# Score products of 512 columns into two sums, with three shared PSUM banks instead of four

## The chip, the cores and the metric

The kernel runs on one core of a Trainium2 chip. The metric is the device time of one execution in microseconds (us), the median of several runs. A profiled execution beside them shows the work of each engine: PE (TensorE), whose weight loads are listed as PEld, DVE (VectorE), ACT (ScalarE), POOL (GpSimd), and SP, which only issues transfers here.

## The reference

For each of four batches, q, k and v are 6336 rows of 256 channels. The columns of q and k are normalised over the rows, a 256 by 256 score matrix is formed, its softmax is applied to v, and a gated convolution of five taps follows.

```python
qn = q / (np.linalg.norm(q, axis=1, keepdims=True) + 1e-06)
kn = k / (np.linalg.norm(k, axis=1, keepdims=True) + 1e-06)
s = kn.transpose(0, 2, 1) @ qn / tau          # 256 x 256 a batch
s = s - s.max(-1, keepdims=True)
a = np.exp(s)
a /= a.sum(-1, keepdims=True) + 1e-09
x = v @ a
# gate: a causal convolution of x over five rows, a weight for each tap and channel
gate = 1.0 / (1.0 + np.exp(-gate_pre))
val = x @ w_val
out = gate * val @ w_out
```

All of it is float32.

## The kernel before

There are two kinds of work, and they run interleaved. The **score side** of a batch reads q and k in groups of three row tiles (128 rows each). For most groups each number is split into a high part (`hi`, rounded to the fast float32r format of the PE, by ACT) and a low part (the rest, by POOL), and the score is summed on the PE from three products of 256 columns for each row tile and each half of the channels: high times high, high times low, low times high. A few early groups skip the split and use slower float32 products of the raw data. ACT squares the rows, and DVE and POOL add the squares up (`acc`, L214) for the norms. The sum of the scores is one PSUM tile, `s_ps`, opened by a product with zeros (`clear`, L231).

The **value side** works on chunks of 508 rows (the last one of a batch has 240), 52 steps in all. A step transposes a chunk of v on the PE (`t_ps`, two tiles), which ACT and DVE split into `v_hi` (L336) and `v_lo` (L337); multiplies it with the softmax weights (`x_ps`, two tiles), from which ACT and then DVE form the five taps of the gate (L359, L361); takes the sigmoid (L367); multiplies it with softmax times `w_val` (`val_ps`, two tiles), which DVE multiplies into the gate (L374); splits that again (L387, L388), multiplies it with `w_out` (`o_ps`, two tiles) and copies the result out (L414). Each step of the pipeline works for a different chunk: in one turn the PE computes `val_ps` of a chunk, `x_ps` of the next, `t_ps` of the one after, and `o_ps` of the one before.

When a batch's scores are complete, `softmax` (L236 on) runs as a chain of small instructions on PE, ACT and DVE between those of the value side. Its tile of norms, called `o_ps` as well (L245), stays in use until the reciprocal of the exponentials' sum (L272). For batch 2 its first product starts at 337.94 us and that reciprocal at 356.86 us.

**PSUM** has eight banks. Before the change `s_ps` holds one, the running sums `acc_ps` one, `x_ps` two, and the other four are shared in turn (tag "bank") by `t_ps`, `val_ps`, `o_ps` and the tiles of softmax. A tile takes a bank that is free again, so its first product waits until the last reader of the tile that had this bank is done.

The order of the work on each engine is set when the kernel is built, by a scheduler that weighs the instructions by a model of their times. Each engine then executes its own list strictly in that order. Any edit to pools or tiles makes new lists.

## Time and profile before

| | |
|---|---|
| median of 3 runs | 657.26 us (657.15 to 657.44) |
| the profiled execution's own time | 658.18 us |
| its span, first to last instruction | 656.3 us |
| PE busy | 637.8 us, 97% of the span |
| DVE, ACT, POOL busy | 80%, 71%, 55% |
| score products of split parts (L226) | 852 of 256 columns |

A line of the profile that groups instructions names the source line, engine, operation, the tiles as out<-in, the shape and the count; behind the first bar stand the busy time in us and the mean duration of one in ns, and behind the second the idle time of that engine just before them and what ended it. Products on the PE are pipelined: the duration of one is longer than the distance from its start to the next one's, and it is the distance that the PE pays.

### The profile page before, as it was taken

The page shows a single profiled execution, that of the slowest core. Times are in us where ns is not written, and L with a number is a line of the kernel's source. Part 1 is how long each engine was busy: PE and PEld are TensorE (multiplying, and loading weights), DVE is VectorE, ACT ScalarE, POOL GpSimd, SP SyncE. Part 2 cuts the span into 40 slices and gives each one's busy share as a digit, 9 for nine tenths or more (in the row PEclk, how much of TensorE's full clock was granted, in tenths as well). Part 3 has the DMA queues.
Part 4 walks back from the last instruction along what each step waited for, and adds up shares of the span by engine and source line. Part 5 has one row for each costly group of instructions (what it writes and reads, how often), then busy time and mean ns, then how long its engine had stood idle before and what let it go on. Part 6 is the DMA issues. An engine that isn't in the chain of part 4 may idle for free.

```text
span 656.3 us, 10656 instructions
## 1 busy us (share of the span) xinstructions
PE 637.8 (97%) x4008; PEld 571.1 (87%) x4008; DVE 523.0 (80%) x832; ACT 466.1 (71%) x607; POOL 360.8 (55%) x173
## 2 busy tenths in 40 slices
PE   7989999999999999999998999999999999999996
PEld 5868799989979999999997998998999798888886
DVE  3898689787878688778788688778778888888894
ACT  4565978867888768668698687767777756655564
POOL 2442796965837769659565497766763222312220
PEclk9999999999999999999999999999999999999999
DMA  8999874555635565545564365563222343443213
GB/s 268 322 328 337 267 225 152 161 166 165 179 103 176 188 195 176 173 132 170 175 184 121 109 217 158 189 185 104 65 78 71 118 126 95 121 129 104 65 50 100
DMA packets 107875, 105.75 MB, mean 161 GB/s; under 512 B 5744, under 2 KB 107312, under 8 KB 107824
## 3 DMA queue, kind: packets, MB, share of 16 engines
q1 hardware_dynamic: 81520, 79.24, 39.0%
q10 hardware_dynamic: 26304, 25.84, 13.9%
q8 instruction: 31, 0.51, 0.3%
q14 instruction: 20, 0.16, 0.1%
HBM read 79.11 MB, written 25.95 MB: 160 GB/s over the span
## 4 chain that ended last, share of the span: by engine, by line
PE 85%; ACT 5%; DVE 4%; POOL 2%; DMA 2%; issue 1%; SPq 1%; ACTq 0%; POOLq 0%
PE o_ps L404 20%; PE x_ps L345 20%; PE val_ps L345 19%; PE s_ps L226 18%; PE t_ps L335 6%; POOL hi L193 1%; ACT sq L209 1%; PE o_ps L294 1%; DMA raw<-in_k_dram 1%; DVE acc_ps L214 1%; ACT hi L192 1%; DVE gate L361 1%; DMA v_raw<-in_v_dram 1%; DVE gate L374 1%; ACT gate L367 0%
## 5 line engine op out<-in xcount | busy, mean ns | idle before, releaser
L361 DVE SCALAR_TENSOR_TENSOR gate<-x_ps,wa,gate 128x508 f32<-128x508 f32 (+1 forms) x416 | 275.4, 716 | 15.7 <-ACT gate L359 14.6
L193 POOL TENSOR_TENSOR hi<-raw,hi 128x1536 fp32r<-128x1536 f32 (+2 forms) x54 | 167.8, 3110 | 94.5 <-ACT hi L192 94.5
L388 POOL TENSOR_TENSOR g_lo<-gate,g_hi 128x1016 fp32r<-128x1016 f32 (+1 forms) x50 | 116.6, 2332 | 145.2 <-ACT g_hi L387 130.6
L214 DVE TENSOR_TENSOR acc_ps<-acc_ps,sq 128x512 f32<-128x512 f32 (+1 forms) x134 | 93.4, 697 | 74.8 <-ACT sq L209 71.6
L345 PE MATMUL x_ps<-v_hi,w 128*128 128x512 f32 (+1 forms) x416 | 139.1, 394 | 0.0
L345 PE MATMUL val_ps<-v_hi,w 128*128 128x508 f32 (+1 forms) x416 | 133.9, 383 | 0.8 <-ACT o_sb L414 0.7
L226 PE MATMUL s_ps<-hi 128*128 128x256 f32 (+1 forms) x852 | 121.1, 287 | 7.4 <-ACT hi L192 4.0
L226 PEld LDWEIGHTS s_ps<-hi 128*128 128x128 f32 (+1 forms) x852 | 110.7, 190 | 13.9 <-ACT hi L192 5.5
L404 PE MATMUL o_ps<-wo_hi,g_hi 128*128 128x256 f32 x400 | 113.2, 283 | 1.7 <-ACT g_hi L383 1.5
L414 ACT COPY o_sb<-o_ps 128x512 f32<-128x512 f32 x99 | 58.2, 589 | 79.1 <-PE o_ps L404 77.9
L404 PE MATMUL o_ps<-wo_lo,g_hi 128*128 128x256 f32 x400 | 112.1, 280 | 0.0
L404 PE MATMUL o_ps<-wo_hi,g_lo 128*128 128x256 f32 x400 | 111.7, 280 | 0.0
L209 ACT ACTIVATE sq<-raw 128x1536 f32<-128x1536 f32 (+3 forms) x69 | 96.0, 1393 | 16.5 <-DVE acc_ps L214 7.9
L214 POOL TENSOR_TENSOR acc<-acc,sq 128x512 f32<-128x512 f32 x58 | 76.4, 1318 | 39.7 <-ACT sq L209 39.3
L345 PEld LDWEIGHTS x_ps<-v_hi,w 128*128 128x128 f32 x416 | 78.2, 190 | 14.3 <-DVE gate L361 0.2
L345 PEld LDWEIGHTS val_ps<-v_hi,w 128*128 128x128 f32 x416 | 77.1, 188 | 14.5 <-ACT o_sb L414 0.9
L359 ACT ACTIVATE gate<-x_ps,wa 128x508 f32<-128x508 f32 (+1 forms) x104 | 68.2, 671 | 20.5 <-PE x_ps L345 20.2
L336 ACT CAST v_hi<-t_ps 128x512 fp32r<-128x512 f32 (+1 forms) x104 | 55.8, 569 | 36.2 <-PE t_ps L335 36.2
L345 PE MATMUL x_ps<-v_lo,w 128*128 128x512 f32 (+1 forms) x208 | 80.2, 386 | 0.0
L345 PE MATMUL val_ps<-v_lo,w 128*128 128x508 f32 (+1 forms) x208 | 79.2, 381 | 0.0
L374 DVE TENSOR_TENSOR gate<-val_ps,gate 128x508 f32<-128x508 f32 (+1 forms) x104 | 64.3, 657 | 18.3 <-ACT gate L367 14.0
L404 PEld LDWEIGHTS o_ps<-wo_hi,g_hi 128*128 128x128 f32 x400 | 75.2, 188 | 3.1 <-ACT g_hi L383 1.7
(84 smaller groups left out, 799.3 us busy)
## 6 DMA issues: line engine op xcount, KB each, us to landing
raw<-in_q_dram SPq DMA_DIRECT2D x64, 384.0 KB
raw<-in_k_dram SPq DMA_DIRECT2D x64, 384.0 KB
v_raw<-in_v_dram SPq DMA_DIRECT2D x44, 512.0 KB
out_dram<-o_sb ACTq DMA_DIRECT2D x48, 384.0 KB
out_dram<-o_sb ACTq DMA_DIRECT2D x48, 124.0 KB
v_raw<-in_v_dram SPq DMA_DIRECT2D x4, 384.0 KB
raw<-in_q_dram SPq DMA_DIRECT2D x4, 128.0 KB
raw<-in_k_dram SPq DMA_DIRECT2D x4, 128.0 KB
```

The source lines that it names most:

```text
L193: nc.gpsimd.tensor_tensor(hi[r, js, :, 1, :], raw[r, js, :, :], hi[r, js, :, 0, :].bitcast(F32), ALU.subtract)
L209: nc.scalar.activation(sq[0:np_, ja:jb], raw[0:np_, ja:jb], AF.Square)
L214: eng.tensor_tensor(st[key][0:np_], st[key][0:np_], sq[0:np_, j], ALU.add)
L226: nc.tensor.matmul(st["s"][:, h, :], lhs, rhs, start=False, stop=stop and h == NH - 1 and n_ == len(ops) - 1)
L336: nc.scalar.copy(th[:, h, 0:w], tp[:, 0:w])
L345: nc.tensor.matmul(ps, wt[:, which, ws, ch, hs], vs[:, ch, lo:hi_], start=n_ == 0, stop=n_ == 3 * NH - 1)
L359: nc.scalar.activation(gate[:, h, 0:w], x_ps[:, 0:w], AF.Copy, scale=cw[:, h, 0:1])
L361: nc.vector.scalar_tensor_tensor(gate[:, h, 0:w], x_ps[:, tap:tap + w], cw[:, h, tap:tap + 1], gate[:, h, 0:w], ALU.mult, ALU.add)
L374: nc.vector.tensor_tensor(gate[:, h, 0:w], val_ps[:, 0:w], gate[:, h, 0:w], ALU.mult)
L388: nc.gpsimd.tensor_tensor(gl[:, :, 0:w], gate[:, :, 0:w], gh[:, :, 0:w].bitcast(F32), ALU.subtract)
L404: nc.tensor.matmul(o_ps[:, u * C:(u + 1) * C], gs[:, h, off:off + P], ws[:, h, :], start=n_ == 0, stop=n_ == 3 * NH - 1)
L414: marks["ACT"] = nc.scalar.copy(o_sb[:, j:j + len(pair), :], o_ps[:, 0:len(pair) * C].rearrange("p (j c) -> p j c", c=C))
```

## The change

The two products that share the high half of k become one: `hi` of k is loaded once and multiplied with 512 columns, the high and the low part of q side by side. Its result goes to 512 columns of a sum, the first half holding high times high, the second high times low. The low part of k times the high part of q, 256 columns, is added to the first half. So each half of the channels now has a bank of its own, `s_ps` holds two banks instead of one, and the shared pool has three instead of four. `clear` becomes two products. At the end ACT copies the second half out, as it copied the whole before, and one new DVE instruction adds the first half to it. The handle that is kept in `marks["PE"]` is overwritten by softmax before it is read.

```diff
-    ps = ctx.enter_context(tc.tile_pool(name="ps", bufs=4, space=PSUM))
+    ps = ctx.enter_context(tc.tile_pool(name="ps", bufs=3, space=PSUM))
...
-                s=ps_s.tile([P, NH, C], F32, name="s_ps"),
+                s=ps_s.tile([P, NH, 2 * C], F32, name="s_ps"),
...
-                    ops = [(hi[r, j, 1, x, hs], hi[r, j, 0, y, :]) for x, y in ((0, 0), (0, 1), (1, 0))]
+                    ops = [(hi[r, j, 1, 0, hs], hi[r, j, 0, :, :].rearrange("p x c -> p (x c)")),
+                           (hi[r, j, 1, 1, hs], hi[r, j, 0, 0, :])]
                 for n_, (lhs, rhs) in enumerate(ops):
-                    nc.tensor.matmul(st["s"][:, h, :], lhs, rhs, start=False,
-                                     stop=stop and h == NH - 1 and n_ == len(ops) - 1)
+                    marks["PE"] = nc.tensor.matmul(st["s"][:, h, 0:rhs.shape[1]], lhs, rhs, start=False,
+                                                   stop=stop and n_ == len(ops) - 1)
...
-            nc.tensor.matmul(st["s"].rearrange("p h c -> p (h c)"), zeros[:, 0:P], zeros, start=True, stop=False)
+            for h in range(NH):
+                nc.tensor.matmul(st["s"][:, h, :], zeros[:, 0:P], zeros, start=True, stop=False)
...
-        nc.scalar.copy(s, st["s"])
+        nc.scalar.copy(s, st["s"][:, :, C:])
+        nc.vector.tensor_tensor(s, st["s"][:, :, 0:C], s, ALU.add)
```

The scheduler makes new lists from this. Three places of them follow; the numbers in the names tell the tiles apart, and "waits" names the engines whose signals an instruction waits for (DMAHW is a transfer). Line numbers of the changed kernel stand up to three higher behind the edits.

The first place is the PE in a step amid the scores of batch 2. Before the change, the two transposed tiles (2949 and 2956) of a step stand one behind the other, ahead of the step's `x_ps`:

```order
L345 MATMUL val_ps_2935<-v_hi_2699,w_1876 128x508
L335 MATMUL t_ps_2949<-ident_96,v_raw_2746 128x128 [waits DMAHW1_49,Activation_49]
L335 MATMUL t_ps_2949<-ident_96,v_raw_2746 128x128 x3
L335 MATMUL t_ps_2956<-ident_96,v_raw_2746 128x128 [waits Activation_49]
L335 MATMUL t_ps_2956<-ident_96,v_raw_2746 128x128 x3
L345 MATMUL x_ps_2903<-v_hi_2823,w_1876 128x512 [waits DVE_49]
```

In the changed kernel the second one (2813) comes after both `x_ps` and ten of the twelve score products of a group:

```order
L227 MATMUL s_ps_1616<-hi_2750 128x256
L227 MATMUL s_ps_1616<-hi_2750 128x512
L227 MATMUL s_ps_1616<-hi_2750 128x256
L338 MATMUL t_ps_2813<-ident_96,v_raw_2615 128x128 [waits DVE_49]
L338 MATMUL t_ps_2813<-ident_96,v_raw_2615 128x128 x3
L227 MATMUL s_ps_1616<-hi_2750 128x512
L227 MATMUL s_ps_1616<-hi_2750 128x256
L407 MATMUL o_ps_2821<-wo_hi_111,g_hi_2682 128x256 [waits DVE_49]
```

The score products now alternate between 512 and 256 columns, and some of them stand between the first transposed tile and the second.

The second place is the PE during the softmax of batch 1, where the tile of norms (o_ps_1628) holds one of the three banks. Here both transposed tiles and then `o_ps` follow one another directly:

```order
L227 MATMUL s_ps_1616<-hi_1619 128x512
L227 MATMUL s_ps_1616<-hi_1619 128x256
L338 MATMUL t_ps_1690<-ident_96,v_raw_1453 128x128 [waits DMAHW0_49,DVE_49]
L338 MATMUL t_ps_1690<-ident_96,v_raw_1453 128x128 x3
L338 MATMUL t_ps_1697<-ident_96,v_raw_1453 128x128 [waits DVE_49]
L338 MATMUL t_ps_1697<-ident_96,v_raw_1453 128x128 x3
L407 MATMUL o_ps_1707<-wo_hi_111,g_hi_1520 128x256 [waits DVE_49]
L407 MATMUL o_ps_1707<-wo_lo_112,g_hi_1520 128x256
```

Before, the first transposed tile stood some 25 products earlier at this place, and with four banks `o_ps` had another bank to take than those of the two. With the norms in one of three, the tiles 1690 and 1697 take the other two, and o_ps_1707 takes the bank of 1690.

The third place is DVE at the same time in the changed kernel, from the second multiplication of the gate (`val_ps`) to the two `v_lo` that read the transposed tiles:

```order
L377 TENSOR_TENSOR gate_1479<-val_ps_1667,gate_1479 128x508 [waits PE_49]
L261 RECIPROCAL o_ps_1628<-o_ps_1628 128x256 [waits DVE_49]
L364 SCALAR_TENSOR_TENSOR gate_1633<-x_ps_1634,wa_109,gate_1633 128x508 [waits Activation_49]
L263 TENSOR_SCALAR nk_1678<-o_ps_1628,rtau_107 128x2 [waits DVE_49]
L364 SCALAR_TENSOR_TENSOR gate_1633<-x_ps_1646,wa_109,gate_1633 128x508 [waits Activation_49]
L364 SCALAR_TENSOR_TENSOR gate_1633<-x_ps_1634,wa_109,gate_1633 128x508 [waits DVE_49]
L266 SCALAR_TENSOR_TENSOR s_1610<-s_1610,nk_1678,o_ps_1628 128x256 [waits DVE_49]
L266 SCALAR_TENSOR_TENSOR s_1610<-s_1610,nk_1678,o_ps_1628 128x256
L364 SCALAR_TENSOR_TENSOR gate_1633<-x_ps_1646,wa_109,gate_1633 128x508 [waits DVE_49]
L340 TENSOR_TENSOR v_lo_1689<-t_ps_1690,v_hi_1688 128x512 [waits Activation_49]
L364 SCALAR_TENSOR_TENSOR gate_1633<-x_ps_1634,wa_109,gate_1633 128x508 [waits DVE_49]
L340 TENSOR_TENSOR v_lo_1689<-t_ps_1697,v_hi_1688 128x512 [waits Activation_49]
```

Four taps, a reciprocal over 256 columns, two scalings of the scores and one small instruction stand between that multiplication and the first `v_lo`. In the softmax of batch 2 these are three taps and the row minimum (L268), in that of batch 3 one small instruction, three taps, two scalings and the row minimum; at both places the PE's list has the same order as above, two transposed tiles and then two `o_ps`.

## The prediction

> **What bounds the kernel now.** I read the page's engine totals and its chain first, then the stretches between and during the softmaxes, then the waits inside those.
>
> ```profile
> PE 637.8 (97%) x4008; PEld 571.1 (87%) x4008; DVE 523.0 (80%) x832; ACT 466.1 (71%) x607; POOL 360.8 (55%) x173
> PE 85%; ACT 5%; DVE 4%; POOL 2%; DMA 2%; issue 1%; SPq 1%; ACTq 0%; POOLq 0%
> ```
>
> The PE is busy nearly all the time, and 85% of the chain that ended last is its own work. So every us taken from its list counts, and so does every wait put into it. The table of stretches (start:end, length, then busy time of PE, PEld, DVE, ACT, POOL, granted clock, DMA) tells where it waits:
>
> ```profile
> 100.00:180.00 80.00, 80.00 (x532) 72.87 (x531) 66.05 (x102) 62.58 (x77) 57.36 (x25) 1.00 0.54 160
> 215.00:330.00 115.00, 115.00 (x778) 105.66 (x778) 92.00 (x146) 84.67 (x104) 80.02 (x35) 1.00 0.55 167
> 360.00:490.00 130.00, 130.00 (x868) 119.13 (x867) 101.18 (x161) 96.86 (x119) 90.05 (x40) 0.99 0.46 139
> 545.00:640.00 95.00, 95.00 (x580) 84.43 (x579) 83.18 (x128) 54.73 (x83) 26.41 (x11) 1.00 0.33 96
> 180.00:215.00 35.00, 34.21 (x214) 29.78 (x214) 28.93 (x50) 29.48 (x43) 20.59 (x9) 1.00 0.52 153
> 330.00:360.00 30.00, 27.31 (x172) 24.41 (x171) 24.10 (x42) 26.97 (x38) 17.82 (x9) 0.97 0.57 164
> 490.00:525.00 35.00, 33.75 (x204) 29.34 (x203) 29.63 (x50) 26.31 (x41) 11.75 (x6) 1.00 0.33 94
> ```
>
> The first four stretches lie between softmaxes and after the last: the PE never rests. The last three hold the softmaxes of batches 1, 2 and 3: 0.8, 2.7 and 1.25 us of rest. These are the sensitive places, since the norms occupy a shared bank there.
>
> **The products.** An instruction's price on the PE is the distance between starts:
>
> ```profile
> 299.62 2.43 PE L226 MATMUL s_ps<-hi 128*128 128x256 f32 x19
> 301.89 0.28 PE L404 MATMUL o_ps<-wo_hi,g_hi 128*128 128x256 f32 x1
> 302.01 0.28 PE L404 MATMUL o_ps<-wo_lo,g_hi 128*128 128x256 f32 x1
> ...
> 310.48 0.40 PE L345 MATMUL x_ps<-v_hi,w 128*128 128x512 f32 x1
> ...
> 313.01 0.40 PE L345 MATMUL x_ps<-v_hi,w 128*128 128x512 f32 x1
> ```
>
> Nineteen products of 256 columns take 301.89 - 299.62 = 2.27 us, 0.1195 each. Between the first and the last of the quoted run of twelve products of 512 columns lie eleven distances, 313.01 - 310.48 = 2.53 us, 0.230 each. Three of 256 cost 0.3585, one of 512 and one of 256 cost 0.3495: 0.009 us saved per triple. The number of columns stays the same; only a fixed part of one instruction goes. The 852 products are 284 triples: **-2.5 us** (0 if the 512 columns cost as two of 256). In the Trainium skill, the section "Wait — 56ns, not 53.3ns?" of "TensorE: Matmul & The Clock Gate" gives a fixed cost of about 2.5 ns per product, by which the saving would be 284 x 2.5 ns = 0.7 us, an estimate from that page. The rows here show a larger fixed part, and I keep theirs.
>
> `clear` gains one product of 512 columns in each batch: 4 x 0.230 = **+0.9 us**.
>
> **The new addition on DVE** reads PSUM and 512 elements per partition, as these do:
>
> ```profile
> L240 DVE TENSOR_TENSOR acc_all<-acc_ps,acc 128x512 f32<-128x512 f32 x4 | 2.7, 682 | 0.1
> PE s_ps L231 <- ACT s L242: 0.7, 1, 0.7
> PE val_ps L345 <- ACT o_sb L414: 0.7, 1, 0.7
> ```
>
> Four times 0.68 us. The next batch's `clear` must now wait for it instead of ACT's copy. Before, the PE waited for that copy once for 0.7 us (the second row), after batch 0, where little else is ready: there the addition is on the path, **+0.7 us**. In the other three softmaxes value-side products cover `clear`; without that cover each would cost up to 0.68 us more, 2 us in all.
>
> **The bank in the steady steps.** A step asks for six shared tiles, and before the change a fourth bank was in use when the second `t_ps` came. The new list puts both `x_ps` and ten score products (4.5 us) ahead of it, so `val_ps` has that long to be read. The step's DVE work is shorter than the step (92.00 us of 115.00 in the second stretch), so I take 0 for the steps with scores. After 545 us there are no score products to put between, and DVE is busy 83.18 of 95 us. There the second `o_ps` product group follows right when the second multiplication of the gate ends; I take 0.1 us for each of 12 steps, **+1 us**, between 0 and 6 (0.5 each, about one instruction of DVE).
>
> **The bank during softmax** is the main term. With the norms in one bank two are left. The PE's list has t, t, o, o, so the first `o_ps` waits for the first `v_lo`, on the bank of the first `t_ps`; and that `t_ps` waits for the multiplication that reads `val_ps`. Between that multiplication and `v_lo`, DVE works through the items in its list while the PE has only the rest of two transposes. Before, the DVE list of batch 2 has the same items here:
>
> ```profile
> 350.06 1.28 DVE L374 TENSOR_TENSOR gate<-val_ps,gate 128x508 f32<-128x508 f32 x2 [0.30 <-ACT gate L367]
> 351.26 0.74 DVE L361 SCALAR_TENSOR_TENSOR gate<-x_ps,wa,gate 128x508 f32<-128x508 f32 x1
> 351.91 0.68 DVE L265 TENSOR_REDUCE m<-s 128x2 f32<-128x512 f32 x1
> 352.51 1.39 DVE L361 SCALAR_TENSOR_TENSOR gate<-x_ps,wa,gate 128x508 f32<-128x508 f32 x2
> 353.82 0.68 DVE L337 TENSOR_TENSOR v_lo<-t_ps,v_hi 128x512 fp32r<-128x512 f32 x1
> L258 DVE RECIPROCAL o_ps<-o_ps 128x256 f32<-128x256 f32 x4 | 7.1, 1763 | 0.1
> L263 DVE SCALAR_TENSOR_TENSOR s<-s,nk,o_ps 128x256 f32<-128x256 f32 x8 | 3.5, 473 | 0.0
> L260 DVE TENSOR_SCALAR nk<-o_ps,rtau 128x2 f32<-128x2 f32 x4 | 0.8, 208 | 0.0
> 585.74 1.03 PE L335 MATMUL t_ps<-ident,v_raw 128*128 128x128 f32 x8
> 586.53 0.48 PE L345 MATMUL x_ps<-v_hi,w 128*128 128x512 f32 x1
> ```
>
> The columns of a timeline row are start and duration in us. From the end of the second multiplication (350.06 + 1.28 = 351.34) to the end of `v_lo` (353.82 + 0.68 = 354.50) pass 3.16 us: three taps, the row minimum, `v_lo`. Eight transposes take 586.53 - 585.74 = 0.8 us, 0.4 a tile.
>
> - Batch 2, the same items: 3.16 us, of which the PE fills 0.4 with the second `t_ps`: 2.7 us of waiting.
> - Batch 3 adds the small instruction and the two scalings: 3.16 + 0.21 + 0.95 = 4.3, less 0.4: 3.9 us.
> - Batch 1 has a fourth tap (about 0.7, half of the 1.39 us of two), the reciprocal, the small instruction and the scalings, and no row minimum: 3.16 + 0.7 + 1.76 + 0.21 + 0.95 - 0.68 = 6.1. Adding up the PE's list, the PE gets to its first `t_ps` when the second multiplication ends, so both transposes lie inside: 5.3 us.
>
> Together **+11.9 us**. Batch 0 has no `o_ps` group at its softmax, so 0 there. In the list of before nothing waits here: the first transposed tile is written earlier and a fourth bank is free for `o_ps`. From below this term is bounded by 0, if `v_lo` were ready when the PE comes; from above by the same waits without any transpose beside them, 13.6 us.
>
> **Further waits** follow in the same stretches, since the softmax tiles go on using banks. In batch 1 a transposed tile of the next step waits for a multiplication that stands behind an addition of squares, for which ACT must first cast a whole group:
>
> ```profile
> L192 ACT CAST hi<-raw 128x1536 fp32r<-128x1536 f32 x44 | 65.0, 1479 | 0.0
> ```
>
> One such wait in each of the three, a cast and a reader, is 1.48 + 0.68 = 2.2 us, 6.5 in all. The rest of 4.75 us that the PE had in these stretches will partly fall into them; I count half of it off: **+4 us**, between 0 and 9.
>
> **The clock.** Before, one long rest of the PE was followed by slow products:
>
> ```profile
> 354.89 0.28 PE L404 MATMUL o_ps<-wo_hi,g_lo 128*128 128x256 f32 x1
> 357.86 0.53 PE L226 MATMUL s_ps<-hi 128*128 128x256 f32 x1 [2.69 <-ACT hi L192]
> 358.19 0.63 PE L345 MATMUL x_ps<-v_hi,w 128*128 128x512 f32 x1
> 358.62 0.63 PE L345 MATMUL x_ps<-v_lo,w 128*128 128x512 f32 x1
> 358.00:361.50 3.50, 3.50 (x9) 2.78 (x10) 1.72 (x3) 3.47 (x5) 3.50 (x2) 0.52 0.36 90
> ```
>
> After 2.69 us of idleness the granted clock is 0.52 for about 3.5 us and a product of 512 columns takes 0.43 us instead of 0.23: 3.5 x 0.48 = 1.7 us lost. The new rests of batches 1 and 3 are longer than that one, so two more such spells are likely, 3.4 us, part of which falls before another wait: **+2 us**, between 0 and 3.4. The Trainium skill, in Part 1 of "TensorE: Matmul & The Clock Gate", puts the clock back to half after an idle window of about 3.4 us that runs freely; by that the rest of batch 2 need not slow anything and those of batches 1 and 3 may. The trace shows it after 2.69 us, and I go by the trace.
>
> **Sum**: -2.5 + 0.9 + 0.7 + 1 + 11.9 + 4 + 2 = +18 us. The profiled execution's own time is 658.18 us (its span of 656.3 and 1.9 around it), which gives 676.2. It lies 0.9 us above the median of the runs shown, so the forecast for the median is **675.3 us**, 2.7% slower.
>
> **Rivals.**
>
> *The lists cover the missing bank.* The scheduler placed `t_ps` elsewhere in the steady steps, and if the PE comes late to those `o_ps`, behind other waits, `v_lo` is done. Then only the products and `clear` count: 657.26 - 2.5 + 0.9 = 655.7 us, 0.2% faster. It decides if fewer than two instructions of DVE stand in front of `v_lo` when the PE arrives. For it: before, the PE never rests over 325 us between softmaxes in which banks are shared too, and its one listed wait for a shared bank is 0.7 us (the last row with the addition). Against it: the lists have four to eight instructions there, and the PE's list has nothing between. Chance 0.08. If the addition and the 512-column products are a little dearer than I think, the same case ends within 0.2% (about what a measurement of this kernel can tell from no change): 0.04.
>
> *The waits are there but half as long*, because the PE reaches the transposes later, behind waits for POOL's low parts, and the long rests then cause no slow clock: -2.5 + 0.9 + 0.7 + 6 + 1 = +6 us, 663.4 us. For it: two of the three stretches already have rests of their own. Against it: a later PE comes later to everything. Chance 0.13.
>
> *The bank is short in every step.* If a `val_ps` is read later than its next tile is due, each turn slips. For it: after 545 us DVE has only 12 of 95 us free, and a `t_ps` takes the bank of a `val_ps` there. Against it: the PE list gives 4.5 us of other products. At half a us in each of 46 steps it is 23 us on top of the sum: 698 us. Chance 0.06.
>
> *The change does not do what it says*: it does, as the rows of the lists show 512 and 256 columns in turn; a 512-column product that costs two of 256 would raise the sum by 2.5 us and nothing else.
>
> **How the numbers follow.** The sum has 0.69, its own range from the lower and upper ends of its terms is 664 to 686 us. With the milder case taken in from below and some of the steady one from above, 661 to 688 holds 8 in 10. Slower by over 0.2%: 0.69 + 0.13 + 0.06 = 0.88; the same: 0.04; faster: 0.08.
>
> **What would show it.** In the profile after, the group of L227 should hold 284 products of 512 columns and 284 of 256; the stretches between softmaxes should stay without rest of the PE. The waits should list `o_ps` L407 on the PE as ended by DVE `v_lo` L340, three times with 2.5 to 5.5 us, each in a softmax, and two more spells of half clock. The prediction is wrong if these waits are below 1 us, if the PE rests in the steady steps, or if the whole loss sits at the addition L245 and the `clear` behind it.

## The result and the profile after

The changed kernel takes **686.78 us** (median of 4 runs, 685.12 to 688.84), against 657.26 before: a ratio of 1.0459 as recorded, with a 95% interval of 1.0436 to 1.0482 (the two medians alone divide to 1.0449). The forecast was 675.3 us with a range of 661 to 688. So the direction was right and the time lies just inside the range, 11.5 us above the forecast. It lies above the 664 to 686 us that the prediction gave as the range of its sum alone. The profiled span grew from 656.3 to 684.2 us, by 27.9.

The totals of the engines and the chain that ended last, after:

```profile
PE 648.0 (95%) x3728; PEld 560.2 (82%) x3728; DVE 526.0 (77%) x836; ACT 470.9 (69%) x607; POOL 360.3 (53%) x173
PE 66%; DVE 11%; ACT 11%; issue 4%; SPq 3%; DMA 2%; POOL 2%; ACTq 1%; DVEq 0%
```

The PE's own share of the chain fell from 85% to 66%, and DVE's rose from 4% to 11%: the end is no longer set by the PE's work alone but by work that the PE waits for. The products themselves changed as described. The groups of L227, shapes kept apart:

```profile
L227 PE MATMUL s_ps<-hi 128*128 128x512 f32 x280 | 104.3, 406 | 6.0 <-POOL hi L193 6.0
L227 PE MATMUL s_ps<-hi 128*128 128x256 f32 x280 | 78.5, 280 | 0.0
```

(Four more of each cover 64 rows, so there are 284 of each, as forecast.) The stretches after, cut at the starts of the steps (columns as in the table of the prediction):

```profile
179.70:236.50 56.80, 50.95 (x292) 44.88 (x292) 42.04 (x71) 40.91 (x56) 29.27 (x14) 0.94 0.47 139
236.50:355.40 118.90, 118.45 (x710) 103.52 (x709) 93.62 (x148) 89.28 (x109) 82.55 (x37) 1.00 0.56 167
355.40:418.10 62.70, 57.96 (x350) 50.17 (x349) 47.25 (x81) 48.60 (x65) 37.93 (x16) 1.00 0.50 153
418.10:514.70 96.60, 96.14 (x576) 84.15 (x574) 77.27 (x120) 72.19 (x86) 67.01 (x29) 1.00 0.40 119
514.70:579.50 64.80, 57.60 (x335) 50.25 (x335) 48.56 (x83) 38.77 (x61) 12.46 (x6) 0.95 0.31 94
579.50:664.20 84.70, 84.51 (x502) 72.19 (x501) 71.82 (x110) 48.56 (x72) 21.36 (x10) 1.00 0.31 91
```

The first, third and fifth hold the softmaxes of batches 1, 2 and 3. The PE rests 5.9, 4.7 and 7.2 us in them (length less busy), and the granted clock falls to 0.94 and 0.95 in the first and the last of these. The steady stretches between them rest little, 0.45 us each in the second and the fourth, where before they did not rest at all.

Where the 27.9 us came from is read most safely from the starts of the same work in both traces. The table below gives, for each stretch between the starts of `val_ps` of two steps (steps counted from 0, the place of a softmax named), the length before and the growth of the changed kernel. It stands here once for all runs, and the experiments come back to it.

```
growth in us against before, between the first products of val_ps
kernel                     to    0-8   8-12  12-22  22-27  27-35  35-41  41-50   50 to   all
                       step 0         batch 1       batch 2       batch 3          end
length before            76.3   99.6   49.9  117.7   61.0   95.9   55.0   82.2   18.7  656.3
the change               +2.7   +1.0   +6.9   +1.1   +1.8   +0.7   +9.8   +2.5   +1.3  +27.9
three banks alone        -0.2   +0.2   +5.9   +1.3   +1.7   +0.6   +7.6   +0.1   +1.4  +18.7
three banks, norms out   +1.6   +0.7   +1.1   +1.6   +2.9   +0.7   +2.9   +2.7   +1.4  +15.7
change, no addition      +2.3   +0.5   +3.1   +1.0   +0.5   +0.6   +6.9   +0.1   +1.0  +15.9
change, small addition   +2.2   +1.1   +3.4   +1.1   +3.7   +0.6   +9.9   +2.8   +1.3  +26.1
change, added in SBUF    +1.8   +2.9   +6.0   +1.2   +2.8   +0.6  +10.6   +2.6   +1.0  +29.4
change, 256 columns      +2.5   +1.1   +9.4   +1.3   +1.7   +0.6   +5.1   +0.1   +1.4  +23.2
change, norms out        +3.0   +2.2   +2.5   +2.0   +4.0   +0.7   +4.1   +2.7   +1.3  +22.5
before, norms out        +1.2   +1.3   -1.4   +0.0   -0.3   -0.0   -1.4   +0.1   -0.1   -0.6
change, five in a pool  +11.2   +2.6   +5.9   +3.3   +0.1   +4.6   +9.4   +8.4   -1.2  +44.2
```

Each row rests on one execution. Executions of the same kernel differ by up to some 4 us in all (the changed kernel's four runs lie between 685.12 and 688.84 us), so tenths of a us in a single place say little. The first column is the least safe. Its length depends on when the first softmax begins, and that varies where the lists do not: up to ACT's copy of batch 0's sum, the kernel before, three banks alone and the two that only move the norms have equal lists, and the copy starts at 55.13, 53.04, 54.60 (three banks, norms out) and 56.19 us (before, norms out). The change, the kernel without the addition and the one with the small addition have equal lists up to there too. Counted from that copy, in us:

```
                             before  three banks  no addition  small addition  the change
ACT's copy of the sum starts  55.13        53.04        55.25           54.64       53.61
val_ps of step 0 starts       76.33        76.16        78.59           78.49       79.06
between                       21.20        23.12        23.34           23.85       25.45
```

So the change lost 4.3 us between copy and step 0, and the table shows 2.7, because its execution came to the copy 1.5 us sooner. The mark at the end of this stretch has a flaw as well: before, only two products of `val_ps` run at 76.33 and the third waits until 78.24, while with three banks all run one behind the other. Some 1.3 us of the growth up to step 0 is therefore paid back in the next column, and steps 0 to 8 grew by more than the table shows.

Batches 1 and 3 hold 16.7 of the 27.9 us. The waits after, on the PE and on its weight loads:

```profile
PE o_ps L407 <- DVE v_lo L340: 8.8, 6, 3.3
PE t_ps L338 <- DVE gate L377: 4.5, 8, 1.9
PEld t_ps L338 <- DVE gate L377: 9.4, 17, 2.2
```

The numbers are the total, the count and the longest. These are the two kinds that the prediction named for a missing bank: `o_ps` behind `v_lo`, and `t_ps` behind the multiplication that reads `val_ps`. Before, no `o_ps` waited for `v_lo`.

At the softmax of batch 1, DVE's and then the PE's rows, after:

```profile
184.26 1.28 DVE L377 TENSOR_TENSOR gate<-val_ps,gate 128x508 f32<-128x508 f32 x2 [1.66 <-ACT gate L370]
185.46 1.75 DVE L261 RECIPROCAL o_ps<-o_ps 128x256 f32<-128x256 f32 x1
187.13 0.67 DVE L364 SCALAR_TENSOR_TENSOR gate<-x_ps,wa,gate 128x508 f32<-128x508 f32 x1
187.71 0.20 DVE L263 TENSOR_SCALAR nk<-o_ps,rtau 128x2 f32<-128x2 f32 x1
187.84 1.39 DVE L364 SCALAR_TENSOR_TENSOR gate<-x_ps,wa,gate 128x508 f32<-128x508 f32 x2
189.15 0.86 DVE L266 SCALAR_TENSOR_TENSOR s<-s,nk,o_ps 128x256 f32<-128x256 f32 x2
189.93 0.74 DVE L364 SCALAR_TENSOR_TENSOR gate<-x_ps,wa,gate 128x508 f32<-128x508 f32 x1
190.58 0.68 DVE L340 TENSOR_TENSOR v_lo<-t_ps,v_hi 128x512 fp32r<-128x512 f32 x1
```

```profile
185.73 1.75 PE L227 MATMUL s_ps<-hi 128*128 128x512 f32 x8
187.41 1.09 PE L338 MATMUL t_ps<-ident,v_raw 128*128 128x128 f32 x8
191.31 0.58 PE L407 MATMUL o_ps<-wo_hi,g_hi 128*128 128x256 f32 x1 [2.81 <-DVE v_lo L340]
191.70 0.42 PE L407 MATMUL o_ps<-wo_lo,g_hi 128*128 128x256 f32 x1
...
196.39 0.41 PE L407 MATMUL o_ps<-wo_hi,g_lo 128*128 128x256 f32 x1
...
205.12 0.66 PE L338 MATMUL t_ps<-ident,v_raw 128*128 128x128 f32 x4 [1.93 <-DVE gate L377]
```

DVE does exactly the items that the prediction listed, and the PE's `o_ps` begins 0.05 us after `v_lo` ends (190.58 + 0.68 = 191.26). Between 191.70 and 196.39 lie 22 distances of 0.213 us where 0.1195 was the price: a spell of half clock, 22 x 0.0935 = 2.1 us lost. The same at batch 3, twice:

```profile
524.63 0.58 PE L407 MATMUL o_ps<-wo_hi,g_hi 128*128 128x256 f32 x1 [3.33 <-DVE v_lo L340]
525.01 0.41 PE L407 MATMUL o_ps<-wo_lo,g_hi 128*128 128x256 f32 x1
...
527.97 0.28 PE L407 MATMUL o_ps<-wo_hi,g_hi 128*128 128x256 f32 x1
...
538.25 0.54 PE L348 MATMUL x_ps<-v_hi,w 128*128 128x244 f32 x1 [2.19 <-DVE gate L364]
...
539.14 0.41 PE L407 MATMUL o_ps<-wo_lo,g_hi 128*128 128x256 f32 x1
...
541.48 0.32 PE L407 MATMUL o_ps<-wo_hi,g_hi 128*128 128x256 f32 x1
```

From 525.01 to 527.97 are 14 distances, 2.96 us instead of 1.67; from 539.14 to 541.48 eleven, 2.34 instead of 1.31. The granted clock (the column behind the engines) in short stretches behind these three rests and, in the second row, behind the rest at 205.12:

```profile
190.00:194.50 4.50, 3.19 (x15) 3.19 (x16) 4.50 (x9) 1.26 (x4) 0.00 (x0) 0.50 0.44 111
205.00:209.00 4.00, 3.88 (x27) 3.60 (x28) 4.00 (x8) 1.53 (x2) 2.40 (x1) 1.00 0.96 300
525.00:529.00 4.00, 4.00 (x24) 4.00 (x24) 3.58 (x8) 1.92 (x5) 0.00 (x0) 0.64 0.00 0
537.00:541.00 4.00, 2.75 (x11) 2.54 (x12) 3.96 (x8) 1.04 (x1) 1.09 (x1) 0.64 0.39 131
```

### The profile page after: what moved, and what is told of

Read it like the earlier page. It is cut to its first block, busy times and chain, and to the rows that moved or that the text cites. A ratio compares the mean times of both kernels' runs of the same rounds, so it can differ in the third digit from the quotient of the medians.

```text
span 684.2 us, 10086 instructions
## 1 busy us (share of the span) xinstructions
PE 648.0 (95%) x3728; PEld 560.2 (82%) x3728; DVE 526.0 (77%) x836; ACT 470.9 (69%) x607; POOL 360.3 (53%) x173
## 4 chain that ended last, share of the span: by engine, by line
PE 66%; DVE 11%; ACT 11%; issue 4%; SPq 3%; DMA 2%; POOL 2%; ACTq 1%; DVEq 0%
PE o_ps L407 20%; PE val_ps L348 14%; PE x_ps L348 14%; PE s_ps L227 13%; PE t_ps L338 5%; DVE acc_ps L214 3%; ACT sq L209 3%; DVE gate L364 3%; ACT hi L192 3%; SPq L74 2%; DVE gate L377 2%; POOL hi L193 2%; ACT gate L370 1%; DMA w_raw<-in_moe_w_out_dram 1%; ACT L370 1%
## 5 line engine op out<-in xcount | busy, mean ns | idle before, releaser
L364 DVE SCALAR_TENSOR_TENSOR gate<-x_ps,wa,gate 128x508 f32<-128x508 f32 (+1 forms) x416 | 280.0, 715 | 29.8 <-ACT gate L362 28.1
L214 DVE TENSOR_TENSOR acc_ps<-acc_ps,sq 128x512 f32<-128x512 f32 (+1 forms) x134 | 93.4, 697 | 89.0 <-ACT sq L209 85.9
L348 PE MATMUL val_ps<-v_hi,w 128*128 128x508 f32 (+1 forms) x416 | 136.7, 383 | 1.4 <-DVE w L302 1.4
L407 PE MATMUL o_ps<-wo_hi,g_hi 128*128 128x256 f32 x400 | 118.6, 297 | 10.6 <-DVE v_lo L340 8.8
L227 PE MATMUL s_ps<-hi 128*128 128x512 f32 (+1 forms) x568 | 114.6, 343 | 6.0 <-POOL hi L193 6.0
L407 PE MATMUL o_ps<-wo_lo,g_hi 128*128 128x256 f32 x400 | 114.4, 286 | 0.0
L407 PE MATMUL o_ps<-wo_hi,g_lo 128*128 128x256 f32 x400 | 114.0, 285 | 0.0
L227 PEld LDWEIGHTS s_ps<-hi 128*128 128x128 f32 x568 | 88.2, 188 | 21.5 <-POOL hi L193 9.5
L214 POOL TENSOR_TENSOR acc<-acc,sq 128x512 f32<-128x512 f32 x58 | 76.5, 1319 | 37.1 <-ACT sq L209 36.7
L407 PEld LDWEIGHTS o_ps<-wo_hi,g_hi 128*128 128x128 f32 x400 | 77.6, 194 | 16.9 <-DVE v_lo L340 10.3
L339 ACT CAST v_hi<-t_ps 128x512 fp32r<-128x512 f32 (+1 forms) x104 | 58.3, 568 | 31.9 <-PE t_ps L338 30.9
L377 DVE TENSOR_TENSOR gate<-val_ps,gate 128x508 f32<-128x508 f32 (+1 forms) x104 | 64.7, 656 | 17.7 <-ACT gate L370 8.8
```

The costliest lines, as they stand in the source:

```text
L214: eng.tensor_tensor(st[key][0:np_], st[key][0:np_], sq[0:np_, j], ALU.add)
L227: marks["PE"] = nc.tensor.matmul(st["s"][:, h, 0:rhs.shape[1]], lhs, rhs, start=False, stop=stop and n_ == len(ops) - 1)
L339: nc.scalar.copy(th[:, h, 0:w], tp[:, 0:w])
L348: nc.tensor.matmul(ps, wt[:, which, ws, ch, hs], vs[:, ch, lo:hi_], start=n_ == 0, stop=n_ == 3 * NH - 1)
L364: nc.vector.scalar_tensor_tensor(gate[:, h, 0:w], x_ps[:, tap:tap + w], cw[:, h, tap:tap + 1], gate[:, h, 0:w], ALU.mult, ALU.add)
L377: nc.vector.tensor_tensor(gate[:, h, 0:w], val_ps[:, 0:w], gate[:, h, 0:w], ALU.mult)
```

## The experiments

Theory: the third bank costs, most of all because the norms hold one of three through softmax. Rivals: the merged products or the second sum cost by themselves; the new addition on DVE does; the remade lists do, whatever part of the change remade them.

**The third bank alone.** The kernel before, with one shared bank less and nothing else changed.

```diff
-    ps = ctx.enter_context(tc.tile_pool(name="ps", bufs=4, space=PSUM))
+    ps = ctx.enter_context(tc.tile_pool(name="ps", bufs=3, space=PSUM))
```

> The kernel before with one edit: three shared banks instead of four (one bank stays empty); products, sums and softmax as before. Bank theory (the loss of the change comes from the missing fourth bank, for the most part while the norms hold one of three): about the time of the changed kernel, since that kernel's products and its addition cancel but for a few us: 680 to 692 us. Rival (the loss comes from the new DVE addition, the longer wait of the next clear and the products): within 2 us of before, 657 us.

Measured: 677.58 us, ratio 1.0311 (1.0290 to 1.0331), 20 us of the change's 29.5. That is a little under the 680 to 692 us named for the bank and far from the rival's 657. The growth sits at batches 1 and 3, 5.9 and 7.6 us, and little of it in the steady steps (third row of the table).

**The norms out of the bank, in the change.** The square root writes the norms to SBUF, so their bank is free as soon as it has been read.

```diff
+        nm = soft_p.tile([P, C + 2 * NH], F32, name="nm")
-        r, rk, z = n_ps[:, 0:C], n_ps[:, C:C + NH], n_ps[:, C + NH:C + 2 * NH]
-        marks["ACT"] = nc.scalar.activation(n_ps[:, 0:C + NH], n_ps[:, 0:C + NH], AF.Sqrt)
+        r, rk, z = nm[:, 0:C], nm[:, C:C + NH], nm[:, C + NH:C + 2 * NH]
+        marks["ACT"] = nc.scalar.activation(nm[:, 0:C + NH], n_ps[:, 0:C + NH], AF.Sqrt)
...
-        nc.vector.tensor_scalar(n_ps[:, 0:C + NH], n_ps[:, 0:C + NH], 1e-6, None, ALU.add)
+        nc.vector.tensor_scalar(nm[:, 0:C + NH], nm[:, 0:C + NH], 1e-6, None, ALU.add)
```

> The changed kernel, three shared banks, but the square root writes the norms to SBUF and the reciprocals and scalings work there, so the bank of the norms is free after one ACT instruction instead of about 20 us later. Bank theory, with the norms as the main holder: the growth at the softmaxes of batches 1 to 3 (some 17 us) goes for the most part, 668 to 674 us. If the third bank is missing everywhere alike: 680 to 686 us. Rival (addition, clear, products): 685 to 688 us.

Measured: 680.59 us, ratio 1.0350 (1.0328 to 1.0373), 6.2 us less than the change. The 668 to 674 us named for the norms are missed, and the time falls among the 680 to 686 named for a bank that is missing everywhere alike; by place, though, it is not alike everywhere. Batches 1 and 3 fall from 6.9 and 9.8 to 2.5 and 4.1 us, 10.1 together; 4.7 of that is given back, 2.2 of it at batch 2. The same edit in the kernel before is the control:

> The kernel before, four shared banks, with the norms moved to SBUF by the square root as in the run of the change with that edit: its control. Bank theory: with four banks the held one costs little, 654 to 659 us. If the edit is good or bad for another reason than the bank, it shows here with the same sign and size as there (-6 us).

Measured: 655.76 us, ratio 0.9969 (0.9956 to 0.9981): within 0.3% of the kernel before, as expected. With four banks the norms' bank costs no more than 1.4 us at batch 1 and 1.4 at batch 3. The 2.5 us that come back before step 8 are in part the later start of this execution (its copy of the first sum came 1.1 us later, with equal lists up to there).

**The norms out of the bank, three banks, nothing of the change.** The edit above in the kernel with three banks.

> The kernel before with three shared banks and the norms moved to SBUF by the square root, so that the norms' bank is free at once; nothing else of the change. If the norms that hold one of three banks through softmax cost the 13.9 us that batches 1 and 3 grew by with three banks alone, most of it goes, as in the change with early norms (two thirds): 664 to 670 us against 677.6. If three banks cost in all steps, or the list, 675 to 679.

Measured: 673.55 us, ratio 1.0238 (1.0208 to 1.0268), 4.0 us less than three banks alone; the expectation of 664 to 670 is missed. At the two places it named, it held: 5.9 and 7.6 fall to 1.1 and 2.9 us, 9.5 of 13.5. The stretches and the wait, with three banks alone first and then with the norms moved:

```profile
176.00:231.80 55.80, 51.10 (x319) 45.35 (x319) 40.51 (x70) 41.00 (x57) 29.31 (x14) 0.97 0.49 144
510.00:572.60 62.60, 57.41 (x334) 50.22 (x334) 47.26 (x80) 38.78 (x61) 10.74 (x5) 0.95 0.32 97
PE o_ps L404 <- DVE v_lo L337: 6.9, 5, 3.0
```

```profile
178.30:229.30 51.00, 49.06 (x320) 43.93 (x320) 40.69 (x70) 41.18 (x58) 29.34 (x14) 1.00 0.52 158
509.10:567.00 57.90, 55.00 (x335) 47.40 (x335) 47.66 (x81) 38.72 (x61) 12.54 (x6) 1.00 0.36 104
PE o_ps L405 <- DVE v_lo L338: 1.3, 2, 1.0
```

The waits of `o_ps` for `v_lo` fall from 6.9 to 1.3 us and the clock in both softmaxes is back at 1.00. But 6.5 us come back elsewhere: 1.8 before step 0, 0.5 up to step 8, 0.3 in steps 12 to 22, 1.2 at batch 2 and 2.6 in the last stage. Nothing in this edit touches the last stage, which has no softmax; only its lists are new. Of the 1.8 us before step 0, 1.6 had passed before the first softmax, where the lists of both kernels are equal: that part is a difference of two executions. So about half of the gain was taken back with the remade lists. That the norms' hold is the cause at batches 1 and 3 rests on two pairs, each with remade lists: the six kernels with three shared banks and the norms in one of them grow by 3.1 to 9.4 us at batch 1 and 5.1 to 10.6 at batch 3, the two with the norms out by 1.1 and 2.5, and by 2.9 and 4.1. The groups do not overlap, but their nearest members lie only 0.6 and 1.0 us apart. The waits of `o_ps` for `v_lo` make the stronger case: with the norms out they fall in both pairs, here from 6.9 to 1.3 us and in the change from 8.8 to 1.6.

**The products not merged.** The change with the three products of 256 columns, high times low into the second bank; addition and both clears stay.

```diff
-                    ops = [(hi[r, j, 1, 0, hs], hi[r, j, 0, :, :].rearrange("p x c -> p (x c)")),
-                           (hi[r, j, 1, 1, hs], hi[r, j, 0, 0, :])]
+                    ops = [(hi[r, j, 1, x, hs], hi[r, j, 0, y, :]) for x, y in ((0, 0), (0, 1), (1, 0))]
...
+                    c0 = C if n_ == 1 else 0
+                    marks["PE"] = nc.tensor.matmul(st["s"][:, h, c0:c0 + C], lhs, rhs, start=False,
```

> The changed kernel with the merged product taken apart again: three products of 256 columns, the one of high times low into the second bank of the sum; two banks for the sum, two clears, the addition and three shared banks stay. If merging is worth its price on the PE, 284 times 0.009 us, this is 2 to 3 us slower than the change: 688 to 690 us. If the 9 us by which the change is slower than three shared banks alone come from the merged products, it returns to about 678 us.

Measured: 682.09 us, ratio 1.0370 (1.0354 to 1.0385): 4.7 us *faster* than with the products merged, and neither of the two times named. In the table it loses 2.5 us more at batch 1 and gains 4.7 at batch 3 and 2.4 in the last stage, places where there are few score products or none. The saving of 2.5 us per execution is real on the PE (the distances after are 0.233 and 0.117 us, 0.350 a triple against 0.3585), but it is smaller than what one set of lists differs from another. The traces also show which pair is the closer one. Without the score products, the PE's weight loads of this kernel are those of three banks alone, in the same order but for three blocks of 4, 12 and 2 that moved, while the change orders, for one, the whole last stage otherwise. So this run against three banks alone comes nearest to the price of the second sum with its clears and its addition: 4.5 us, where the prediction's prices give 1.6.

**Without the addition.** The change without the DVE addition; high times low is left out of the result.

```diff
-        nc.scalar.copy(s, st["s"][:, :, C:])
-        nc.vector.tensor_tensor(s, st["s"][:, :, 0:C], s, ALU.add)
+        nc.scalar.copy(s, st["s"][:, :, 0:C])
```

> The changed kernel without the DVE addition: ACT copies the first halves of the sums out and the second halves (high of k times low of q) are left out of the result; everything else as in the change. Theory that the addition delays the next clear: the growth of 2.7 us before the first value product (softmax of batch 0) goes, and perhaps 1 to 2 us later, 681 to 684 us. Rival (the list or the second clear does it): within 1 us of the change.

Measured: 674.56 us, ratio 1.0254 (1.0238 to 1.0269), 12.2 us less than the change and 3.0 less than three banks alone; neither of the two expectations had this. In the first column 2.3 of 2.7 us stay, but from ACT's copy on, batch 0 takes 2.1 us less than in the change (the small table). By this pair the addition costs 12 us where the prediction had 0.7. The lists differ from the first softmax on, so the pair alone cannot say whether the instruction or the lists cost it. Two more runs do.

**A small addition at the same place.** The addition covers 4 of the 256 columns of each half.

```diff
-        nc.scalar.copy(s, st["s"][:, :, C:])
-        nc.vector.tensor_tensor(s, st["s"][:, :, 0:C], s, ALU.add)
+        nc.scalar.copy(s, st["s"][:, :, 0:C])
+        nc.vector.tensor_tensor(s[:, :, 0:4], st["s"][:, :, C:C + 4], s[:, :, 0:4], ALU.add)
```

> The change, but the new DVE instruction adds only 4 of the 256 columns of each half (the rest of the high times low part is left out of the result). It stands at the same place, waits for the same things and is waited for by the same clear, but should last some 0.1 to 0.2 us instead of 0.68. The lists of the PE and DVE are those of the change, row for row, up to the softmax of batch 1; of POOL and SP all through. If the addition costs its own duration on the path (four times some 0.5 us, and what follows from it), 682 to 685 us is the most that it can give back directly and the growth of 2.7 us at batch 0 falls to about 2.2. If the 12 us by which the kernel without the addition is faster came from its duration, 675 to 677. If they came from the lists that the planner makes with and without it, 683 to 688, with 2.2 to 2.7 us of growth at batch 0.

Measured: 685.45 us, ratio 1.0434 (1.0402 to 1.0466), inside the 683 to 688 us named for the lists and not to be told from the change. The tile's row in this run (smallest, median and largest duration in ns):

```profile
L245 DVE TENSOR_TENSOR s<-s_ps,s x4: 146/156/160, 56.3 to 510.6; 128x8 f32<-128x8 f32 x4
```

Each addition is 0.52 us shorter, with lists that are equal up to the softmax of batch 1. At batch 0, in the change:

```profile
55.22 0.68 DVE L245 TENSOR_TENSOR s<-s_ps,s 128x512 f32<-128x512 f32 x1
55.36 0.70 PE L248 MATMUL o_ps<-acc_all,ones 128*128 128x256 f32 x2 [1.79 <-DVE acc_all L242]
57.29 1.20 PE L233 MATMUL s_ps<-zeros 128*128 128x512 f32 x2
58.00:60.00 2.00, 2.00 (x6) 1.19 (x4) 1.89 (x2) 1.99 (x6) 0.04 (x1) 0.50 1.09 347
```

and with the small addition:

```profile
56.27 0.16 DVE L245 TENSOR_TENSOR s<-s_ps,s 128x8 f32<-128x8 f32 x1
56.41 0.70 PE L248 MATMUL o_ps<-acc_all,ones 128*128 128x256 f32 x2 [1.80 <-DVE acc_all L242]
58.14 0.71 PE L233 MATMUL s_ps<-zeros 128*128 128x512 f32 x2
58.00:60.00 2.00, 2.00 (x12) 1.50 (x11) 1.93 (x3) 1.99 (x4) 0.00 (x0) 1.00 1.10 349
```

In neither does the PE wait for the addition. The product for the norms stands ahead of `clear` in its list and waits for the sum of squares, and when the PE comes to `clear` (57.29 in the change) the addition has ended (55.22 + 0.68 = 55.90). What differs is the clock: in the change it falls to half behind the rest of 1.79 us, and from the norms' product to the first transpose that the softmax makes (L288, at 71.71 and 71.16 us) pass 16.35 us instead of 14.75. These 1.6 us belong to this execution's clock and not to the addition.

The span fell by 1.8 us, which looks like four times 0.52, but it did not fall where the additions stand: batch 1 grew by 3.5 us less and batch 2 by 1.9 us more, where the lists differ again. So at most some 2 us of the 12 are the addition's duration; the other 10 between the change and the kernel without it come with the lists, as far as these runs tell. The prediction's own sign of failure, that the whole loss sits at the addition and the clear behind it, did not occur.

**The addition in SBUF.** ACT copies both halves out, and the clear waits for ACT alone.

```diff
-        nc.scalar.copy(s, st["s"][:, :, C:])
-        nc.vector.tensor_tensor(s, st["s"][:, :, 0:C], s, ALU.add)
+        s2 = soft_p.tile([P, NH, 2 * C], F32, name="s2")
+        nc.scalar.copy(s2, st["s"])
+        nc.vector.tensor_tensor(s, s2[:, :, 0:C], s2[:, :, C:], ALU.add)
```

> The change, but ACT copies both halves of both sums out of PSUM (1024 columns in one instruction) and DVE adds them in SBUF, so the clear of the next batch waits for ACT only, as before the change. If the clear's wait for DVE's addition is what the addition costs, its 12 us go or fall to the 1 to 2 us of the longer copy: 675 to 678 us, and the growth at batch 0 falls from 2.7 to 1 to 1.5 us. If it is the lists, any new list is as good a draw as the others: 677 to 690, and batch 0 decides by whether the clear stands ahead of the norms' product in the list of the PE or behind it.

Measured: 688.05 us, ratio 1.0455 (1.0421 to 1.0489), as expected if the lists decide. The clear's wait for DVE is not what costs either; batch 0 falls to 1.8 us, a little above what was named for that case, and steps 0 to 8 lose 1.9 us more.

**Five banks in one pool.** The change with `x_ps` taken from the shared pool too.

```diff
-    ps = ctx.enter_context(tc.tile_pool(name="ps", bufs=3, space=PSUM))
+    ps = ctx.enter_context(tc.tile_pool(name="ps", bufs=5, space=PSUM))
...
-        x_ps = ps.tile([P, 512], F32, name="x_ps", bufs=2)
+        x_ps = ps.tile([P, 512], F32, name="x_ps", tag="bank")
```

> The changed kernel with x_ps taken into the shared pool: five banks in one pool instead of two for x_ps and three for the rest, the same eight banks in all. Bank theory: the short pool can borrow, so the waits at the softmaxes shrink: 665 to 678 us. Rival (the number of banks does not matter, the addition and products do): 685 to 688 us.

Measured: 701.59 us, ratio 1.0666 (1.0649 to 1.0682). Sharing all five makes it worse by 15 us, which neither expectation had, 8.5 of them before step 0 and 5.9 in the last stage. That the split of the five banks between two pools is the cost is not borne out.

**Four shared banks with the second sum.** The bank came from the sum of squares, whose tile went to SBUF, in the change and, as its control, in the kernel before. The control has four shared banks already, so it takes only the second part of the edit and leaves one bank empty.

```diff
-    ps = ctx.enter_context(tc.tile_pool(name="ps", bufs=3, space=PSUM))
+    ps = ctx.enter_context(tc.tile_pool(name="ps", bufs=4, space=PSUM))
...
-                acc=ps_s.tile([P, 2, C], F32, name="acc_ps"),
+                acc=acc_p.tile([P, 2, C], F32, name="acc_sb", bufs=1),
```

> The changed kernel with its running sums of squares in SBUF instead of PSUM, and the bank that this frees given back to the shared pool, which has four again. To be read against the next run, the same edit without the change. Bank theory: the difference of the two is the products (-2.5 us) and the clear and the addition (+1.6 us), so -3 to +1 us. Rival: the difference stays at +20 to +30 us.

> The kernel before with its running sums of squares in SBUF instead of PSUM, four shared banks, one bank empty: the control of the run before. Both theories: 652 to 665 us, since only the place of one operand of 134 DVE additions changes.

Measured: 742.60 us (1.1307, 1.1277 to 1.1337) and 733.43 us (1.1169, 1.1133 to 1.1206). Both expectations are missed. Moving the sum costs 76 us by itself, which the last section explains: DVE's share of the chain rises to 38% and 40%, and for the steps with scores the pair answers another question than it was made for. With the same banks on both sides the change is still 9.2 us slower; how much of that is lists stays open. The last steps, which have no sums of squares, can still be read: against the kernel before, the change with four shared banks grows by 0.0 us in steps 41 to 50 and by 0.1 behind them, where the change with three grows by 2.5 and 1.3.

## Why the prediction was right in direction and short in size

The forecast by place, in the stretches of the table: I give the products by their number in each, the further waits a third to each softmax, and the two spells of half clock to batches 1 and 3, as the prediction had them.

```
                       to step 0   0-8  8-12 12-22 22-27 27-35 35-41 41-50  50-end   sum
forecast                    +1.1  -0.7  +7.6  -0.7  +3.9  -0.5  +6.2  +1.0     0.0  +18
measured                    +2.7  +1.0  +6.9  +1.1  +1.8  +0.7  +9.8  +2.5    +1.3  +27.9
```

**Products, -2.5, and clears, +0.9: right.** The distances after bear out 0.009 us per triple, and there are four more clears. That is their price on the PE; no pair of runs shows it in the total (unmerged is faster, and the kernel without the addition is 3.0 us below three banks alone with other lists). Nor is all of it paid out, as the steady steps show below.

**The bank in softmax, +11.9 of direct waits: right mechanism, too large.** The six waits of `o_ps` for `v_lo` come to 8.8 us. At batch 1 the DVE part was right: from the end of the second multiplication (185.54) to the end of `v_lo` (191.26) pass 5.7 us, the forecast had 6.1. What failed is "the PE gets to its first `t_ps` when the second multiplication ends": eight score products stood ahead of it, it came at 187.41, 1.9 us later, and waited 2.81 instead of 5.3. At batch 3 it waited 3.33, forecast 3.9. At batch 2 the waits in the stretch (in all, how many, the longest) are:

```profile
PE o_ps L407 <- DVE v_lo L340: 2.5, 3, 1.5
```

Three sum to 2.5, as forecast (2.7), but none exceeds 1.5 us and the clock stayed at 1.00. There the kernel before had its own rest of 2.69 us and a spell of half clock behind it; the new list has neither, which the prediction did not count on. So batch 2 grew by 1.8, not 3.9.

**Further waits, +4, and half clock, +2: right in part, each too small.** In softmax of batch 1, `t_ps` waited 1.93 us for a multiplication (the row at 205.12), and at batch 3 `x_ps` waited 2.19 us for a tap, the first as the step "further waits" described it, if not behind the cast it named. The second is of another kind: `x_ps` has its own two banks, before and after, and waited for DVE's late taps. Three spells of half clock in the softmaxes cost 2.1 + 1.3 + 1.0 = 4.4 us where two with 2 us were forecast, and the one at batch 0 cost 1.6 more. Together the softmaxes of batches 1 to 3 grew by 18.5 us; the forecast had 17.7. This sum was right, its parts partly by errors that cancel.

**The steady steps, 0: the step that failed.** With the saved products the three steady stretches should have shrunk by 1.9 us; they grew by 2.8. The mis-sized term is "I take 0 for the steps with scores", which measured +4.7. The argument was that the PE's list puts ten score products ahead of the second `t_ps`, so that `val_ps` has 4.5 us to be read. That row order is there, and the products did not suffice in some of the steps:

```profile
310.07 2.26 PE L227 MATMUL s_ps<-hi 128*128 128x512 f32 x12
312.56 0.66 PE L338 MATMUL t_ps<-ident,v_raw 128*128 128x128 f32 x4 [0.24 <-DVE gate L377]
```

Only the transposed tile waits, 0.2 to 0.4 us at a time: by the starts of the products, five of the 26 steps lose 0.34 to 0.40 us there, 1.9 us together. Such rests are what "without rest of the PE" in the prediction excluded, and its own test says that it was wrong there. Three banks alone grow by 2.1 us in these steps, with nothing saved there, so not quite half of this term belongs to the bank alone. Part of the other 2.6 us is the saving itself: the unmerged kernel grows by 3.0 us in these steps, hardly more than the change, and loses only 0.8 us to that wait, in four steps with 0.19 to 0.23. Merging shortens the very products that cover the reading of `val_ps`, so 1.1 us of what it saves there returns as a longer wait. Where the rest of the term lies stays open.

**The last stage, +1: 2.5.** Each step loses some 0.2 us, inside the bounds of 0 and 6 that were given. But the bank is not enough for it: with three banks alone, without the addition, and with 256 columns the last stage grows by 0.1 us, in the five other kernels with three shared banks by 2.5 to 2.8. The PE's lists there differ in the same way. In the three, a step runs both `val_ps`, the first `t_ps`, both `x_ps`, the second `t_ps` and `o_ps`; in the five, one `x_ps` stands between the two `val_ps`, so only the other is left between the two `t_ps`. From the first to the second `t_ps` pass 3.19 us with three banks alone (593.78 to 596.97) and 1.83 in the change (602.39 to 604.22): the shorter way no longer covers what must be read before the banks are free.

**The addition, +0.7: not borne out, 0 at batch 0.** The PE does not wait for it there (the rows in the run with the small addition). The growth at batch 0 has other sources. From ACT's copy to step 0 three banks alone already lose 1.9 us, where the prediction had 0 for the bank: `val_ps` has to wait until DVE has read the last tile of softmax, whose bank it takes, and in the change this is a wait of 1.4 us for `w` (L302). Of these 1.9 us some 1.3 are paid back in the next steps. The spell of half clock takes 1.6 us more in the execution that was traced; with the small addition, where there is none, 23.85 us remain, 0.7 over three banks alone. Against these stands the sooner start of 1.5 us.

**The tail, 0: +1.3.** Behind step 50 every kernel here with three shared banks grows by 1.0 to 1.4 us, and the three others with four by -0.1 to 0.1, the change with four among them. So it goes with the bank; which wait makes it is not shown, and the prediction has no term for it.

So the 9.9 us between 18 and 27.9 are put together: steady steps +4.7, batch 0 +1.6, last stage +1.5, tail +1.3, softmaxes +0.8 with rounding. The first two shift against each other with the mark for step 0 (1.3 us), their sum does not. What the prediction lacked is a term for the lists themselves. Six kernels with three shared banks and the norms in one of them run between 674.6 and 688.1 us, though what their instructions differ by is worth some 3 us (the products 2.5, the additions 2, the clears 0.9, partly of opposite sign). That is a spread of 13.5 us, more than the largest single term, and the change's lists lie at its upper end. Half of it, some 7 us to either side, would be a fair estimate of such a term here. The milder rival, 663.4, and the one in which lists cover the bank, 655.7, are both excluded; the severe one, half a us in every step, is too: the steady steps lost 0.18 us each (4.7 us over the 26 steps of the three stretches).

Some luck is in the hit. The prediction calls 664 to 686 us the range "from the lower and upper ends of its terms", but those ends as listed add up to about 656 and 693. The measured 686.78 lies above 686; it is inside the final range only by the share of the severe rival that was taken in from above, and that rival did not happen. One reading on the way was also incomplete: beside the wait of 0.7 us that it calls the only one for a shared bank before the change, the waits list `t_ps` behind the gate's multiplication with 0.4 us.

## What to carry to other kernels

Count PSUM banks as you count time: ask for each long-lived tile which bank it holds and for how long, and what waits in turn for the others; here a tile of norms in one of three banks cost more than the merged products could ever save. When a bank must go, first free the tile that holds one longest, and test the loss of the bank alone before anything else of the change. Where a scheduler remakes the order from any edit, price the edit by its instructions, but give the forecast a spread for the lists, measured from a few edits that should cost nothing. And compare two traces only from a mark up to which their lists are equal: here the first softmax began at times 3 us apart with equal lists.

## What the runs showed of the hardware

**Half clock after rests shorter than expected.** The granted clock fell to half behind PE rests of 2.81, 3.33 and 2.19 us (rows above), the last of them with short rests just ahead; behind the rest of 1.93 us at 205.12 and those of up to 1.5 us at batch 2 it stayed at 1.00. Behind the rest of 1.79 us at 55.36 it fell too, and in the kernel with the small addition, which has the same list up to there, it stayed at 1.00 behind a rest of 1.80. So the length of the last rest alone does not tell whether a spell follows. The Trainium skill, Part 1 of "TensorE: Matmul & The Clock Gate", has an idle window of about 3.4 us; none of these rests reached it, and four slowed the clock.

**An addition on DVE with both inputs in SBUF beside POOL.** With the sum of squares in SBUF instead of PSUM, the same addition took 1712 ns instead of 697 on average. DVE's group of L214 in that kernel, the tile's row (smallest, median, largest duration) and the same group in the kernel before:

```profile
L214 DVE TENSOR_TENSOR acc_sb<-acc_sb,sq 128x512 f32<-128x512 f32 (+1 forms) x134 | 229.4, 1712 | 33.8 <-ACT sq L209 28.2
L214 DVE TENSOR_TENSOR acc_sb<-acc_sb,sq x134: 670/1664/4007, 5.5 to 566.7; 128x512 f32<-128x512 f32 x130, 64x512 f32<-64x512 f32 x4
L214 DVE TENSOR_TENSOR acc_ps<-acc_ps,sq 128x512 f32<-128x512 f32 (+1 forms) x134 | 93.4, 697 | 74.8 <-ACT sq L209 71.6
```

The shortest is as fast as in PSUM, 670 ns, the longest takes 4007; POOL's own additions slow down as well, from 1318 to 1722 ns. DVE goes from 523 to 656 us of busy time, and the kernel from 657 to 733. The Trainium skill, in "SBUF — State Buffer", section "Who interferes with whom", says that a DVE instruction with two SBUF inputs contends with an instruction of GpSimd (POOL here) that reads SBUF, because its second input comes through a read interface that the two share, and it calls the sharing an exclusive lock. The trace agrees. One of the long additions beside POOL:

```profile
118.45 3.52 POOL L193 TENSOR_TENSOR hi<-raw,hi 128x1536 fp32r<-128x1536 f32 x1 [0.55 <-ACT hi L192]
119.78 2.73 DVE L214 TENSOR_TENSOR acc_sb<-acc_sb,sq 128x512 f32<-128x512 f32 x1 [0.57 <-ACT sq L209]
```

It ends at 122.51, 0.55 us after POOL's subtraction ends at 121.97. Of the 134 additions 36 take at most 703 ns; each of the other 98 begins while an instruction of POOL runs and ends 0.55 us after the end of one (0.545 to 0.559). The 22 that no instruction of POOL overlaps take 670 to 693 ns. No run stopped POOL, but the ends leave little room for another cause.
